# A fused attention and FFN kernel: blocks of a row-tile pair stored one by one, activation sums on VectorE, part of a weight difference in a place of its own, q and k staged by turns, statistics put later

## The chip, the cores and the metric

The kernel runs on one core of a Trainium2 chip. The metric is device time in microseconds (us) of one execution; smaller is better. Most executions of one kernel lie within 0.3% of each other. "Span" is the time from the first to the last instruction of the profiled execution, some 2 us less than the device time.

In the lines of the profile PE is TensorE's matmuls, PEld its weight loads, DVE is VectorE, ACT ScalarE, POOL GpSimd and SP SyncE; a q behind the name marks the engine's queue, which issues DMAs or waits. L1114 is a line of the kernel's source; the same statement has other line numbers in other kernels. A line of a timeline gives the start, the time taken, what ran (x3: three of them) and, in brackets, how long the engine sat idle before it and what ended that. A line of waits gives the sum in us, how often, and the longest.

## The reference, cut to what matters

```python
def _attn_ref(q, k, v):                       # 8 batches, 12 heads, 448 rows, 64 per head
    scores = np.matmul(q, k.transpose(0, 1, 3, 2)) / np.sqrt(64)
    attn = np.maximum(scores, 0.0) ** 2 / 448
    return np.matmul(attn, v)

def _moe_ref(x, g_ln, w_ch1, w_ch2):          # x: (8, 448, 768)
    mu = np.mean(x, axis=-1, keepdims=True)
    var = np.mean((x - mu) ** 2, axis=-1, keepdims=True)
    xn = (x - mu) / np.sqrt(var + 1e-06) * g_ln
    ch = np.maximum(xn @ w_ch1, 0.0) @ w_ch2  # 768 -> 3072 -> 768
    return x + ch
```

## The kernel before

While one batch goes through the FFN, the attention of the next is dealt out between its matmuls. A small scheduler inside the program gives each piece of work an assumed cost, chooses an engine for it, and writes every engine's instructions in the resulting order; each engine then works in that order. So every change of a dependency deals the work out anew, far beyond the place of the change.

The words used below: scores are the products of q and k, followed by a relu and a square; h is the FFN's hidden layer; centering subtracts a row's mean, and a scaling by g follows it; an evacuation takes a result of TensorE out of PSUM, on VectorE or ScalarE, and so frees its bank.

The second FFN matrix is cut into four quarters b11, b12, b21, b22. From the third batch on, row tiles are taken in pairs, and a pair is multiplied with seven products (P1 to P7, 12 matmuls each) where the plain way has eight. This needs sums of weights (T1 to T4, made once) and of activations (S1 to S4, made for each pair). T1 is b12 minus b11:

```python
def s_op(u, m, name, part, deps):              # an activation sum, 6 rows of hidden units
    def emit(eng):
        (nc.vector if eng == "DVE" else nc.gpsimd).tensor_sub(o, i0, i1)
    return R.add(("DVE", "POOL"), (540.0, 1700.0), emit, deps, key=-2.9, port=True)

for k in range(0, KH, 3):                      # T1 over b12, all 12 rows
    made["T1", k] = run(b12[:, k:k + 3], b12[:, k:k + 3], b11[:, k:k + 3], True, ...)

def ffn_2(u, m, j, part, parts):               # the single row tile beside a pair (once in each even batch)
    ks = [(k, w2[:, k, j * hd:(j + 1) * hd]) for k in range(K2)]
    if u > 0 and j == 1:                       # b12 is gone: add b11 back, 36 matmuls for 24
        ks = [(k, b11[:, k]) for k in range(KH)] + ks
```

The pair's products share two PSUM banks. VectorE evacuates a bank after each product (`evac`). The blocks C11 and C12 of the first tile are stored together; the blocks C22 and C21 of the second tile go one after the other through one half-tile buffer:

```python
elif key in ("p5", "C21"):
    o_t = o_half.tile([P, hd], fp32, tag="oh")          # one buffer
...
ev = evac("C22", 1, hi, r2, True, [e["p5"]])
half_free[0] = store_tile(u, m + 1, hi, ev, False, lambda: e["o", 1])
...
ev = evac("C21", 1, lo, r2, False, [half_free[0]])      # after C22's store has landed
```

q and k of a batch are loaded by GpSimd into the two halves of a staging tile and then turned by a DMA transpose from SyncE. The statistics of a batch's rows (on VectorE) and their square root (on ScalarE) may run as soon as the rows are there.

## Time and profile before

| | before |
|---|---|
| time, median of four runs | 539.01 us (538.92 to 539.26) |
| TensorE busy | 517.1 of 537.3 us |
| TensorE idle in the first 30 us | 9.55 us |
| TensorE idle from 30 us to the last matmul | 6.54 us |
| after the last matmul | 4.14 us |

TensorE is the bound. The three kinds of idleness are read from the table of stretches, with a cut at 30 us and one at the last evacuation. The first and the last are filling and emptying. The middle is where waits cost; it is 0.05 us more than the prediction's 6.49, which left out the smallest stretches. The prediction below shows the lines.

### The profile page before, as it was taken

The page shows a single profiled execution, that of the slowest core. Times are in us where ns is not written, and L with a number is a line of the kernel's source. Part 1 is how long each engine was busy: PE and PEld are TensorE (multiplying, and loading weights), DVE is VectorE, ACT ScalarE, POOL GpSimd, SP SyncE. Part 2 cuts the span into 40 slices and gives each one's busy share as a digit, 9 for nine tenths or more (in the row PEclk, how much of TensorE's full clock was granted, in tenths as well). Part 3 has the DMA queues.
Part 4 walks back from the last instruction along what each step waited for, and adds up shares of the span by engine and source line. Part 5 has one row for each costly group of instructions (what it writes and reads, how often), then busy time and mean ns, then how long its engine had stood idle before and what let it go on. Part 6 is the DMA issues. An engine that isn't in the chain of part 4 may idle for free.

```text
span 537.3 us, 9903 instructions
## 1 busy us (share of the span) xinstructions
PE 517.1 (96%) x4128; PEld 278.8 (52%) x4128; DVE 341.8 (64%) x617; ACT 231.3 (43%) x370; POOL 125.2 (23%) x137
## 2 busy tenths in 40 slices
PE   4899999999999999999988999999998999999996
PEld 3444455555564455555544545655555455554564
DVE  5988647448987588665686666746668646633253
ACT  5977611134225653366223663346441565124300
POOL 6411600311460123421172010702222012101000
PEclk9999999999999999999999999999999999999999
DMA  9999999897299004990069900992022400231022
GB/s 187 196 189 195 198 188 165 117 142 134 47 186 187 1 2 68 185 152 1 1 115 159 147 2 1 162 190 52 2 47 71 97 1 1 59 67 23 1 60 59
DMA packets 142680, 51.82 MB, mean 96 GB/s; under 512 B 121510, under 2 KB 139436, under 8 KB 142636
## 3 DMA queue, kind: packets, MB, share of 16 engines
q0 software_dynamic: 81072, 25.50, 45.1%
q1 hardware_dynamic: 55724, 14.79, 17.7%
q10 hardware_dynamic: 5840, 10.92, 7.4%
q8 instruction: 32, 0.52, 0.4%
q14 instruction: 12, 0.10, 0.1%
HBM read 51.91 MB, written 11.01 MB: 117 GB/s over the span
## 4 chain that ended last, share of the span: by engine, by line
PE 90%; DVE 5%; DMA 2%; ACT 1%; issue 1%; SPq 0%; ACTq 0%; DVEq 0%
PE f_ps L929 40%; PE f_ps L1114 20%; PE f_ps L1190 16%; PE sc L586 6%; PE ps L648 5%; DVE a L840 1%; DMA f<-in_k_dram 1%; DVE a L610 1%; DMA out_dram<-o_t 1%; DVE o_t L1128 1%; ACT a L595 1%; PE ps L507 1%; DVE t L365 0%; PE f_ps L909 0%; DVE a L849 0%
## 5 line engine op out<-in xcount | busy, mean ns | idle before, releaser
L929 PE MATMUL f_ps<-a,w 128*128 128x448 bf16 x1134 | 220.9, 353 | 1.8 <-DVE o_t L1128 1.1
L929 PEld LDWEIGHTS <-w 128*128 128x128 bf16 x1134 | 108.3, 98 | 110.3 <-issue 12.5
L595 ACT ACTIVATE a<-sc 128x896 bf16<-128x896 f32 x114 | 99.9, 923 | 85.6 <-PE sc L586 79.8
L945 ACT ACTIVATE h<-f_ps 128x448 bf16<-128x448 f32 (+1 forms) x161 | 86.0, 535 | 103.9 <-PE f_ps L929 102.4
L610 DVE TENSOR_TENSOR a<-a 128x896 bf16<-128x896 bf16 x156 | 99.0, 668 | 3.1 <-ACT a L595 2.8
L1114 PEld LDWEIGHTS <-h 128*128 128x128 bf16 x648 | 62.8, 98 | 48.7 <-issue 7.5
L1114 PE MATMUL f_ps<-w,h 128*128 128x384 bf16 x432 | 75.6, 326 | 4.4 <-DVE o_t L1128 4.4
L597 DVE TENSOR_SCALAR a<-sc 128x896 bf16<-128x896 f32 x45 | 48.9, 1087 | 24.5 <-PE sc L586 24.4
L1190 PE MATMUL f_ps<-w,h 128*128 128x384 bf16 x372 | 62.1, 326 | 0.0
L586 PE MATMUL sc<-t 64*64 64x448 bf16 x672 | 48.4, 365 | 3.3 <-ACT a L595 1.6
L1190 PEld LDWEIGHTS <-h 128*128 128x128 bf16 x372 | 36.0, 98 | 25.2 <-issue 1.7
L739 POOL TENSOR_TENSOR sum_t<-sum_t,xT_all 128x384 f32<-128x384 f32 (+2 forms) x25 | 20.4, 815 | 99.0 <-ACT xT_all L363 99.0
L1074 DVE TENSOR_TENSOR x_all<-h 128x768 bf16<-128x768 bf16 x18 | 9.9, 562 | 38.5 <-ACT h L945 38.5
L1128 DVE SCALAR_TENSOR_TENSOR o_t<-f_ps,r_t,x_all 128x384 f32<-128x384 f32 x36 | 22.1, 615 | 18.8 <-PE f_ps L1114 14.9
L586 PEld LDWEIGHTS <-t 64*64 64x64 bf16 x672 | 17.6, 106 | 26.5 <-issue 20.1
L737 POOL TENSOR_TENSOR sum_t<-xT_all 128x384 f32<-128x384 bf16 (+2 forms) x13 | 9.2, 720 | 88.9 <-ACT xT_all L363 88.8
L648 PE MATMUL ps<-a,v_t 64*64 64x448 bf16 x552 | 29.8, 350 | 0.0
L847 ACT ACTIVATE a<-a,g_sb 128x448 bf16<-128x448 bf16 x27 | 16.1, 657 | 31.2 <-DVE a L840 30.1
L1128 DVE SCALAR_TENSOR_TENSOR o_t<-f_ps,r_t,o_t 128x384 f32<-128x384 f32 x27 | 16.6, 615 | 19.4 <-PE f_ps L1114 19.2
L363 ACT CAST xT_all<-ps 128x768 bf16<-128x768 f32 (+2 forms) x33 | 20.2, 622 | 20.1 <-PE ps L648 18.3
L401 POOL DMA_DIRECT2D t<-in_q_dram x12 | 19.3, 1774 | 36.1 <-DMA t<-t 34.6
L648 PEld LDWEIGHTS <-v_t 64*64 64x64 bf16 x672 | 19.7, 107 | 13.4 <-issue 2.8
(91 smaller groups left out, 420.2 us busy)
## 6 DMA issues: line engine op xcount, KB each, us to landing
out_dram<-o_t ACTq DMA_DIRECT2D x38, 192.0 KB, 4.7
v_t<-in_v_dram POOLq DMA_DIRECT2D x16, 336.0 KB, 6.3
w<-in_moe_w_ch_dram POOLq DMA_DIRECT2D x4, 1152.0 KB, 40.0
t<-in_q_dram POOLq DMA_DIRECT2D x12, 336.0 KB, 8.3
t<-in_k_dram POOLq DMA_DIRECT2D x12, 336.0 KB, 10.5
out_dram<-o_t ACTq DMA_DIRECT2D x35, 96.0 KB, 2.2
w<-in_moe_w_ch_dram POOLq DMA_DIRECT2D x4, 768.0 KB, 19.2
w<-in_moe_w_ch_dram POOLq DMA_DIRECT2D x1, 1536.0 KB, 29.2
```

What stands on the lines that cost most here:

```text
L363: nc.scalar.copy(o, i)
L586: nc.tensor.matmul(sc[rows_of(half), r, :S], qkT[b][rows_of(r), 1, s * NPER + pn, rows_of(half)], qT[:, :, pn, rows_of(half)], start=True, ...
L595: nc.scalar.activation(attn[n, s], st[0][:, :, :S], Act.Relu, scale=rc2)
L597: nc.vector.tensor_scalar(attn[n, s], st[0][:, :, :S], rc2, 0.0, op0=Alu.mult, op1=Alu.max)
L610: nc.vector.tensor_mul(attn[n, s], attn[n, s], attn[n, s])
L648: nc.tensor.matmul(av_st[n][half][rows_of(hh)], vt[b][rows_of(half), 2 * pn + hh, s * D:(s + 1) * D], attn[n, s][rows_of(half), hh, :], st ...
L739: nc.gpsimd.tensor_add(s0, s0, x0)
L929: nc.tensor.matmul(st[0], w1[:, ki, ni * P:(ni + 1) * P], xc[b][:, ki, :], start=(i == 0), stop=(i == K1 - 1))
L945: nc.scalar.activation(o, st[0][:, c], Act.Relu)
L1114: nc.tensor.matmul(e["ps", bank], a(k), w(k), start=new and k == 0, stop=k == KH - 1, skip_group_check=True)
L1128: nc.vector.scalar_tensor_tensor(o, e["ps", bank], r, o if more else xm[u, m + tile_n][:, cols], op0=Alu.mult, op1=Alu.add)
L1190: nc.tensor.matmul(o_st["ps"], stat(u, m, ki), w, start=(i == 0), stop=(i == len(ks) - 1))
```

## The change

The intent: take matmuls away where b11 had to be added back, and take away the waits of TensorE in the middle. Cut to its core:

```diff
@@ q and k staged by turns: from batch 4 both use the first half of the staging tile
-                        stage[b][half * T:(half + 1) * T, t]...
+                        stage["cols"][half * T:(half + 1) * T, t if b < 4 else 0]...
-                ld.append(load(dma_ns(6 * S, 256), emit, free, 2000.0))
+                ld.append(load(dma_ns(6 * S, 256), emit, free if t == 0 or b < 4 else [later("turn", b, 0)], 2000.0))
@@ statistics and square root later
-            sto = R.add("DVE", 1400.0, stats, [deps_of[m], ops.get(("st0", b))], key=4.0)
+            sto = R.add("DVE", 1400.0, stats, [deps_of[m], ops.get(("st0", b)), later("h", b, 4) if u > 0 else None], key=4.0)
-        sq = R.add("ACT", 300.0, root, [ops["st", u, m] for m in ms], key=3.0)
+        sq = R.add("ACT", 300.0, root, [ops["st", u, m] for m in ms] + [later("h", b, 14) if u > 0 else None], key=3.0)
@@ seven rows of T1 in the second half of the staging tile, five over b12
-        for k in range(0, KH, 3):
-            made["T1", k] = run(b12[:, k:k + 3], b12[:, k:k + 3], b11[:, k:k + 3], True,
+        for k in range(J):                      # J = 7
+            tw["T1", k] = stage["cols"][:, 1, k]
+        for a, z in ((0, 3), (3, 5), (5, J)):
+            made["T1", a] = run(stage["cols"][:, 1, a:z], b12[:, a:z], b11[:, a:z], True, ...)
+        for k, n in ((J, 3), (J + 3, 2)):
+            made["T1", k] = run(b12[:, k:k + n], b12[:, k:k + n], b11[:, k:k + n], True,
...
-            ks = [(k, b11[:, k]) for k in range(KH)] + ks
+            ks = [(k, b11[:, k]) for k in range(J, KH)] + ks
@@ activation sums on VectorE
-        return R.add(("DVE", "POOL"), (540.0, 1700.0), emit, deps, key=-2.9, port=True)
+        return R.add("DVE", 570.0, emit, deps, key=-2.9, port=True)
@@ blocks stored one by one, C21 in the left half of the first tile's output
-                elif key in ("p5", "C21"):
+                elif key == "p5":
+            e["C11 out"] = store_tile(u, m, lo, ev, False, lambda: e["o", 0][:, lo])
-            o_ring.append(store_tile(u, m, slice(0, d_model), ev, False, lambda: e["o", 0]))
+            e["C12 out"] = store_tile(u, m, hi, ev, False, lambda: e["o", 0][:, hi])
-            ev = evac("C21", 1, lo, r2, False, [half_free[0]])
+            ev = evac("C21", 1, lo, r2, False, [e["C11 out"]])
```

More of the change, by code (lines that the diff above doesn't have):

```diff
@@ L392, in load_qk_cols @@
     def load_qk_cols(b):
-        free = [ops["qk_free", 0]] if b == 2 else [ops["turn", b - 1, x] for x in range(2)]
+        free = [ops["qk_free", 0]] if b == 2 else [later("turn", b - 1, x) for x in range(2)]
         for t, src in enumerate((q, k)):
@@ L398, in emit @@
                 def emit(eng, t=t, src=src, half=half):
-                    if half == 0 and t == 0:
-                        stage[b] = big(STAGE[b], None, t=2, j=J, c=hd)
+                    if half == 0 and t == 0 and b == 2:
+                        stage["cols"] = big(STAGE[b], None, t=2, j=J, c=hd)
                     nc.gpsimd.dma_start(
-                        stage[b][half * T:(half + 1) * T, t].rearrange("p j (h d) -> p j h d", d=D),
+                        stage["cols"][half * T:(half + 1) * T, t if b < 4 else 0].rearrange("p j (h d) -> p j h d", d=D),
                         src[b, half * 6:half * 6 + 6].rearrange("h (p j) d -> p j h d", j=J))
-                ld.append(load(dma_ns(6 * S, 256), emit, free, 2000.0))
+                ld.append(load(dma_ns(6 * S, 256), emit, free if t == 0 or b < 4 else [later("turn", b, 0)], 2000.0))
             ops["c_ld", b, t] = ld
@@ L414, in emit @@
                 nc.sync.dma_start_transpose(
-                    qkT[b][:, t], stage[b][:, t].rearrange("p j c -> p (j c)"))
+                    qkT[b][:, t], stage["cols"][:, t if b < 4 else 0].rearrange("p j c -> p (j c)"))
             ops["turn", b, t] = R.add("SP", 100.0, emit, ops["c_ld", b, t] + [ops[free]],
                                       key=0.0, load=(J * NPER * P, 18.0))
+            now_known(ops["turn", b, t], "turn", b, t)
     w1_view = moe_w_ch1.rearrange("(ko kp) n -> kp ko n", kp=P)
@@ L1035, in make_sums @@
                                         tw["T2", k + i].rearrange("p (o c) -> p o c", o=1), True, [made["T2", k + i]] + d, 5.2)
-        for k in range(0, KH, 3):
-            made["T1", k] = run(b12[:, k:k + 3], b12[:, k:k + 3], b11[:, k:k + 3], True,
+        for k in range(J):
+            tw["T1", k] = stage["cols"][:, 1, k]
+        for a, z in ((0, 3), (3, 5), (5, J)):
+            made["T1", a] = run(stage["cols"][:, 1, a:z], b12[:, a:z], b11[:, a:z], True,
+                                w2_ld + [later("turn", 3, 1)], 5.3)
+        for k, n in ((J, 3), (J + 3, 2)):
+            for i in range(k, k + n):
+                tw["T1", i] = b12[:, i]
+            made["T1", k] = run(b12[:, k:k + n], b12[:, k:k + n], b11[:, k:k + n], True,
                                 done3 + [later("f2_end", 0)], 5.3)
@@ L1101, in ffn_w @@
         bank = "x" if name in ("P1", "P6", "P7", "P4") else "y"
-        w = {"P1": lambda k: b11[:, k], "P2": lambda k: b21[:, k], "P6": lambda k: tw["T2", k], "P5": lambda k: b12[:, k],
+        w = {"P1": lambda k: b11[:, k], "P2": lambda k: b21[:, k], "P6": lambda k: tw["T2", k], "P5": lambda k: tw["T1", k],
              "P7": lambda k: tw["T3", k], "P3": lambda k: b22[:, k], "P4": lambda k: tw["T4", k]}[name]
@@ L1123, in emit @@
                     e["o", 0] = o_t
-                elif key in ("p5", "C21"):
+                elif key == "p5":
                     o_t = o_half.tile([P, hd], fp32, tag="oh")
                     e["o", 1] = o_t
-                o = e["o", 1] if tile_n else e["o", 0][:, cols]
+                o = e["o", 1] if key in ("p5", "C22") else e["o", 0][:, cols]
                 nc.vector.scalar_tensor_tensor(o, e["ps", bank], r, o if more else xm[u, m + tile_n][:, cols],
@@ L1137, in ffn_w @@
             e["S4"] = [s_op(u, m, "S4", x, [op, e["S2"][x]]) for x in range(2)]
-            evac("C11", 0, lo, r1, True, [e["c1"]])
+            ev = evac("C11", 0, lo, r1, True, [e["c1"]])
+            e["C11 out"] = store_tile(u, m, lo, ev, False, lambda: e["o", 0][:, lo])
         elif name == "P6":
@@ L1154, in ffn_w @@
             ev = evac("C12", 0, hi, r1, True, [e["c2"], e["C11"]])
-            o_ring.append(store_tile(u, m, slice(0, d_model), ev, False, lambda: e["o", 0]))
+            e["C12 out"] = store_tile(u, m, hi, ev, False, lambda: e["o", 0][:, hi])
         else:
-            ev = evac("C21", 1, lo, r2, False, [half_free[0]])
+            ev = evac("C21", 1, lo, r2, False, [e["C11 out"]])
             f_banks[:] = [e["C12"], ev]
             f_tags.reverse()
-            half_free[0] = store_tile(u, m + 1, lo, ev, final, lambda: e["o", 1])
+            o_ring.append([e["C12 out"], store_tile(u, m + 1, lo, ev, final, lambda: e["o", 0][:, lo])])
             if m == 3:
@@ L1165, in ffn_w, with part_of @@
                 now_known(op, "f2_end", b)
+    def part_of(u, j, part, parts):
+        n = K2 if u == 0 or j == 0 else K2 + KH - J
+        return slice(part * n // parts, (part + 1) * n // parts)
     def f2_deps(u, m, j, part, parts):
-        n = (K2 if u == 0 or j == 0 else 3 * KH) // parts
         b = 2 * u + (0 if m < 3 else 1)
-        z = min((part + 1) * n, K2) - 1
+        z = min(part_of(u, j, part, parts).stop, K2) - 1
         d = [ops["w2", z], ops["h", b, z]]
@@ L1186, in emit @@
                 o_st["ps"] = o_ps
-            n = len(ks) // parts
-            for i in range(part * n, (part + 1) * n):
-                ki, w = ks[i]
+            for i, (ki, w) in list(enumerate(ks))[part_of(u, j, part, parts)]:
                 nc.tensor.matmul(o_st["ps"], stat(u, m, ki), w, start=(i == 0), stop=(i == len(ks) - 1))
-        op = R.pe(162.5 * len(ks) / parts, emit, f2_deps(u, m, j, part, parts) + (ops["sums", "T1"] if u > 0 and j == 1 else []))
+        run = part_of(u, j, part, parts)
+        op = R.pe(162.5 * (run.stop - run.start), emit, f2_deps(u, m, j, part, parts) + (ops["sums", "T1"] if u > 0 and j == 1 else []))
         if m in (2, 6) and j == 1 and part == parts - 1:
@@ L1300, in f2_steps @@
         return [("f2", u, m, j, p, n) for m in ms for j in range(2)
-                for n in [PARTS if u == 0 or j == 0 else 6] for p in range(n)]
+                for n in [PARTS if u == 0 or j == 0 else 5] for p in range(n)]
     def fw_steps(u, ms):
```

## The prediction

> **What bounds the kernel now.** I read four views in this order: the page's busy line, the table of stretches of 10 us, the waits of TensorE, and the timeline and chain of waits at the stretches that were not full.
>
> ```profile
> PE 517.1 (96%) x4128; PEld 278.8 (52%) x4128; DVE 341.8 (64%) x617; ACT 231.3 (43%) x370; POOL 125.2 (23%) x137
> ```
>
> TensorE works 517.1 of 537.3 us, so all that can be won is matmuls taken away, plus at most 20.2 us of idleness. The columns below are the busy time of PE, PEld, DVE, ACT and POOL in each stretch.
>
> ```profile
> 260.00:270.00 10.00, 9.98 (x97) 5.50 (x98) 7.35 (x14) 3.52 (x5) 0.00 (x0) 1.00 0.09 21
> 270.00:280.00 10.00, 9.49 (x63) 5.40 (x56) 7.92 (x11) 2.89 (x4) 8.31 (x9) 1.00 0.66 130
> 280.00:290.00 10.00, 7.94 (x48) 4.58 (x47) 7.30 (x12) 1.78 (x3) 5.45 (x4) 1.00 1.94 124
> 290.00:300.00 10.00, 8.87 (x56) 4.29 (x54) 3.62 (x7) 4.82 (x7) 0.00 (x0) 1.00 0.98 190
> ...
> 400.00:410.00 10.00, 8.20 (x51) 4.83 (x50) 8.25 (x10) 1.50 (x3) 6.11 (x7) 1.00 0.65 128
> ...
> 490.00:500.00 10.00, 9.32 (x50) 4.71 (x49) 1.91 (x6) 4.97 (x10) 0.00 (x0) 1.00 0.01 2
> ```
>
> From 30 us on, TensorE is full except here and for 0.31 us in 420 to 430. The first 30 us lose 9.55 us (loads and first transposes), the tail 4.13 us (last matmul ends at 533.17). The middle loses 0.51 + 2.06 + 1.13 + 1.80 + 0.31 + 0.68 = 6.49 us. The sum, 20.2, closes the account. The waits of TensorE in the middle name the releasers:
>
> ```profile
> PE f_ps L1114 <- DVE o_t L1128: 4.4, 3, 1.8
> PE f_ps L929 <- DVE o_t L1128: 1.1, 1, 1.1
> PE f_ps L929 <- ACT h L945: 0.7, 1, 0.7
> ```
>
> L1114 are the products of the seven-product scheme on a pair of row tiles, L1128 the evacuations of their banks. So 5.5 us are lost where a product waits for a bank. The timeline shows why, at the second pair of an odd batch (the same pattern comes again at 404 us):
>
> ```profile
> 275.49 3.55 POOL L1074 TENSOR_TENSOR h<-h,x_all 128x768 bf16<-128x768 bf16 x2 [1.37 <-PE f_ps L1114]
> 275.97 1.56 DVE L1074 TENSOR_TENSOR h<-h,x_all 128x768 bf16<-128x768 bf16 x1
> ...
> 277.46 3.25 DVE L840 TENSOR_TENSOR a<-xT_all,sum_t 128x768 bf16<-128x768 bf16 x2
> ...
> 280.64 0.60 DVE L1128 SCALAR_TENSOR_TENSOR o_t<-f_ps,r_t,o_t 128x384 f32<-128x384 f32 x1
> ...
> 281.30 2.11 PE L1114 MATMUL f_ps<-w,h 128*128 128x384 bf16 x12 [1.80 <-DVE o_t L1128]
> ```
>
> GpSimd makes two of the pair's activation sums, 1.8 us each. Beside it VectorE takes 1.56 us for a sum that has a minimum of 0.54 elsewhere, and 1.63 for a centering (L840) that takes 0.96 when alone. The evacuation, fourth in VectorE's order, ends 1.8 us too late. Later in the same stage the chain shows another wait:
>
> ```profile
> 286.82 0.47 ACTq L1228
> ...
> 287.33 5.05 DMA out_dram<-o_t
> ...
> 292.58 0.63 DVE o_t L1128
> ```
>
> The pair's last block shares one half-tile buffer with the block before the last, and waits 5.05 us for its store to land; TensorE loses 1.13 us of that.
>
> **What the Trainium skill says.** (1) "VectorE: DVE Perf Modes", section on the TRN2 errata, gives a matmul max(60, 6+FD) cycles at 2.4 GHz: 390 cycles, 162.5 ns, for 384 columns. The trace agrees: a piece of the chain has 60 of them (L1190) in 9.75 us, 162.5 ns each. The 326 ns in the groups is a latency, not the pitch. (2) "SBUF — State Buffer", section "Who interferes with whom": a VectorE instruction with two SBUF inputs contends with a GpSimd instruction that reads SBUF, and the one issued second blocks. The 1.56 and 1.63 us above agree. (3) "DMA: Bandwidth & Descriptors", "Anatomy of one DMA": about 2 us are fixed, mostly the receipt. The 96 KB stores land 2.2 us after issue in the median here; the 5.05 us came while q and k loads held the DMA engines.
>
> **The change, part by part.**
>
> *Home for seven rows of T1 (b12 minus b11).* Before, T1 overwrote b12, so the single tile of each of the three even batches after the first two had to add b11 back: 36 matmuls for its right half. Seven rows now lie in half of the staging tile, b12 stays whole there, and the half takes 24 + 5 = 29. Comparing the built instruction orders of TensorE confirms 21 fewer matmuls and 101 changes between attention and FFN work in both. 21 x 162.5 ns = **3.41 us**, in stretches where TensorE is full, so it counts whole unless the next FFN waits for its centered input. The gains before that FFN end at 348.9 us and it starts at 352.3; in the tightest of the three, 221.4 and 223.6. The mean moves six matmuls (0.98 us) earlier in the order, so most of the 1.14 us taken from each such tile comes from before it. VectorE's work for T1 hardly changes: 12 rows either way.
>
> *Sums on VectorE.* Five sums leave GpSimd (four beside the two stalls, one at 485 us) and cost VectorE 5 x 0.51 us of pitch, beside a TensorE that needs 8 us per four products. In the new order of VectorE, with pitches from the trace (evacuation 0.54, sum 0.5, centering 0.87), from the end of the first product, t: evacuation 0.54, two sums 1.54, centering 2.41, evacuation of the second product 2.95, done at 3.0; the fourth product needs it at 3.9. Two sums 3.95, a centering 4.82, third evacuation done at 5.4; the fifth product needs it at 5.86. So both waits of 1.80 us should go, and with VectorE back in time also the 0.76 us at 286. Gain 1.80 + 1.80 + 0.76 = 4.36 (the 0.51 us of stretch 270 to 280 are the beginning of the first wait).
>
> *Blocks stored one by one.* The last block goes into the left half of the output tile, whose earlier content was stored some 8 us before; the 1.13 us wait goes. Eighteen more stores of 0.55 us issue time fall on ScalarE's queue (43% busy). At the very end the block before the last sends 96 instead of 192 KB a store: about 0.2 us of tail.
>
> *Statistics later.* The square root now stands behind six more evacuations on ScalarE. At 490.4 us ScalarE sat waiting for statistics and TensorE lost 0.68 us, at 428 another 0.31. Both should go: 0.99.
>
> *q and k staged by turns, from batch 4.* k's load starts only after q's transpose. From the trace: transposes 6.4 us to landing, the two k loads about 13 us together. For batch 5: q's turn starts at 229.0, lands at 235.4, k lands at 248.5, its turn at 255; its first scores are at 268.0. Batches 4, 6 and 7 have 12 to 17 us of slack in the same way. Cost: nothing. GpSimd's row sums queue behind the k loads for up to 8 us, but only the last of three per batch is urgent, 30 us later.
>
> **Sum.** 538.98 - 3.41 (matmuls) - 4.36 (port) - 1.13 (store) - 0.99 (statistics) - 0.2 (tail) = 528.9. This is nearly a floor, since head and tail stay. For new small waits after ScalarE and VectorE were dealt out anew I add 1.2 us, a guess of the size of the small waits seen before: **530.1 us**.
>
> **Rivals.** (a) *The wait moves instead of going.* Five more sums make VectorE's order tighter just where it is fullest (about 8 of 10 us at 270 to 290); if each of the two stages keeps half its wait, 2 to 3 us come back: 532.5. For: VectorE's order is strict and the margins above are 0.4 to 0.9 us. Against: all other pairs already ran their sums there without a wait. (b) *Staging by turns is late.* If k took 26 instead of 13 us, batches 5 to 7 would arrive around or after their first scores and the greedy schedule would stall, up to several us each: 535 or more. Against: transfers of 6 to 13 us in every batch of this trace. (c) *Only the matmuls count*, the idleness being a symptom of something else such as a late mean: 535.4. Against: at 281.30 the wait is for the evacuation itself. (d) *Stores hold up ScalarE.* More issues, each waiting for an older store, delay h and the scores' relu: 1 to 3 us back.
>
> **Range and chances.** The floor is about 528.7, because 9.55 us of head and most of the 4.13 us of tail are untouched; rivals (a) and (d) together end near 533. Eight in ten: 528.9 to 533.0. A gain of 2% would need 528.2, below the floor, so faster by over 2% has 0.04; slower by over 2% would need stalls of 20 us: 0.02; within 2%: 0.94.
>
> **What would show it.** TensorE with 4107 matmuls and about 513.7 us busy; no wait of the pair products above 0.5 us; no GpSimd instruction at the line of the activation sums; centerings near 0.96 us throughout; no evacuation waiting for a store; q and k transposes done 10 us before the scores. It is wrong if scores wait for a transpose, if waits for evacuations total over 2 us, or if the gain stays at 3.4 us.

## The result

The changed kernel takes **530.47 us** (median of four runs, 530.28 to 530.81) against 539.01 us before. The ratio is 0.9842, with a 95% interval of 0.9825 to 0.9859. Ratios here are the mean time of one kernel's fast runs over that of the other's of the same rounds, so they are not quite the ratio of the medians. It is 1.6% faster, within the 2% that counts as the same.

The page's busy line of the changed kernel, then its table of stretches (busy time of PE, PEld, DVE, ACT, POOL): around 280 and 400 us, where before had its largest gaps, and around its own largest, at 363 us:

```profile
PE 513.4 (97%) x4107; PEld 276.9 (52%) x4107; DVE 341.5 (65%) x632; ACT 227.0 (43%) x361; POOL 117.3 (22%) x132
```

```profile
270.00:280.00 10.00, 10.00 (x63) 6.00 (x62) 8.27 (x14) 1.48 (x3) 5.72 (x7) 1.00 1.44 162
280.00:290.00 10.00, 10.00 (x68) 5.44 (x66) 7.13 (x15) 3.60 (x5) 0.00 (x0) 1.00 0.72 116
290.00:300.00 10.00, 9.71 (x84) 4.97 (x83) 6.56 (x13) 7.04 (x12) 4.13 (x4) 1.00 0.88 130
...
350.00:360.00 10.00, 9.77 (x92) 4.75 (x91) 6.54 (x16) 7.70 (x14) 2.45 (x2) 1.00 0.81 132
360.00:370.00 10.00, 9.40 (x51) 4.76 (x50) 5.54 (x9) 5.67 (x11) 2.33 (x3) 1.00 1.43 136
...
400.00:410.00 10.00, 10.00 (x63) 6.03 (x62) 8.36 (x17) 1.23 (x2) 0.00 (x0) 1.00 0.21 55
```

Twenty-one matmuls are gone, and the gaps around 280 and 400 us with them. The waits of TensorE between 30 and 522 us are now only these:

```profile
PE sc L587 <- ACT a L596: 1.1, 4, 0.3
PE f_ps L930 <- DVE h L948: 0.6, 1, 0.6
```

No product (L1122 in the changed kernel, L1114 before) waits for an evacuation (L1136, before L1128) any more. The timeline at the place of the first 1.80 us wait:

```profile
274.03 0.62 DVE L1136 SCALAR_TENSOR_TENSOR o_t<-f_ps,r_t,x_all 128x384 f32<-128x384 f32 x1 [0.27 <-PE f_ps L1122]
...
274.56 1.02 DVE L1082 TENSOR_TENSOR h<-h,x_all 128x768 bf16<-128x768 bf16 x2
275.50 0.95 DVE L841 TENSOR_TENSOR a<-xT_all,sum_t 128x768 bf16<-128x768 bf16 x1
...
276.37 0.61 DVE L1136 SCALAR_TENSOR_TENSOR o_t<-f_ps,r_t,o_t 128x384 f32<-128x384 f32 x1
...
278.70 0.61 DVE L1136 SCALAR_TENSOR_TENSOR o_t<-f_ps,r_t,x_all 128x384 f32<-128x384 f32 x1
```

Two sums now take 1.02 us together and a centering 0.95. The second evacuation starts 2.34 us after the first (the prediction laid it at 2.41), the third ends at 5.28 (predicted 5.4).

The span went from 537.3 to 528.6 us, by 8.7: TensorE's busy time fell by 3.7, its idleness in the middle from 6.54 to 1.77 us (4.77), the head by 0.57, and the tail grew by 0.32. The head is no gain of the change: the two instruction orders of TensorE are the same for the first 150 us, and over all fourteen profiles the head lies between 8.6 and 10.1 us.

### The profile page after: what moved, and what is told of

It is laid out like the page before. It is cut to its first block, busy times and chain, and to the rows that moved or that the text cites. A ratio compares the mean times of both kernels' runs of the same rounds, so it can differ in the third digit from the quotient of the medians.

```text
span 528.6 us, 9882 instructions
## 1 busy us (share of the span) xinstructions
PE 513.4 (97%) x4107; PEld 276.9 (52%) x4107; DVE 341.5 (65%) x632; ACT 227.0 (43%) x361; POOL 117.3 (22%) x132
## 4 chain that ended last, share of the span: by engine, by line
PE 93%; DVE 4%; ACT 1%; DMA 1%; issue 0%; ACTq 0%; DVEq 0%
PE f_ps L930 40%; PE f_ps L1122 23%; PE f_ps L1200 15%; PE sc L587 6%; PE ps L649 5%; DVE a L611 2%; ACT a L596 1%; DVE t L365 1%; DMA f<-in_q_dram 1%; PE ps L508 1%; PE f_ps L910 0%; PE ps L711 0%; DVE st L792 0%; DVE st L791 0%; PE f_ps L508 0%
## 5 line engine op out<-in xcount | busy, mean ns | idle before, releaser
L596 ACT ACTIVATE a<-sc 128x896 bf16<-128x896 f32 x117 | 103.4, 927 | 81.9 <-PE sc L587 75.9
L946 ACT ACTIVATE h<-f_ps 128x448 bf16<-128x448 f32 (+1 forms) x156 | 83.2, 534 | 106.5 <-PE f_ps L930 105.2
L611 DVE TENSOR_TENSOR a<-a 128x896 bf16<-128x896 bf16 x156 | 100.6, 683 | 1.4 <-ACT a L596 1.4
L1122 PEld LDWEIGHTS <-h 128*128 128x128 bf16 x648 | 62.8, 98 | 43.8 <-issue 2.4
L598 DVE TENSOR_SCALAR a<-sc 128x896 bf16<-128x896 f32 x42 | 45.6, 1087 | 41.2 <-PE sc L587 41.1
L1122 PE MATMUL f_ps<-w,h 128*128 128x384 bf16 x369 | 65.2, 326 | 0.0
L1200 PE MATMUL f_ps<-w,h 128*128 128x384 bf16 x351 | 58.7, 326 | 0.0
L1200 PEld LDWEIGHTS <-h 128*128 128x128 bf16 x351 | 33.9, 98 | 23.8 <-issue 1.7
L1136 DVE SCALAR_TENSOR_TENSOR o_t<-f_ps,r_t,x_all 128x384 f32<-128x384 f32 x36 | 22.1, 614 | 18.6 <-PE f_ps L1122 18.3
L401 POOL DMA_DIRECT2D t<-in_k_dram x12 | 20.0, 1901 | 52.7 <-DMA t<-t 52.7
L1217 DVE SCALAR_TENSOR_TENSOR o_t<-f_ps,r_t,x_all 128x384 f32<-128x384 f32 x20 | 12.3, 613 | 26.4 <-PE f_ps L1200 26.3
L1136 DVE SCALAR_TENSOR_TENSOR o_t<-f_ps,r_t,o_t 128x384 f32<-128x384 f32 x27 | 16.6, 614 | 14.8 <-PE f_ps L1122 14.7
L848 ACT ACTIVATE a<-a,g_sb 128x448 bf16<-128x448 bf16 x19 | 11.6, 659 | 30.3 <-DVE a L841 15.1
```

What stands on the lines that cost most here:

```text
L401: nc.gpsimd.dma_start(stage["cols"][half * T:(half + 1) * T, t if b < 4 else 0].rearrange("p j (h d) -> p j h d", d=D), src[b, half * 6:ha ...
L596: nc.scalar.activation(attn[n, s], st[0][:, :, :S], Act.Relu, scale=rc2)
L598: nc.vector.tensor_scalar(attn[n, s], st[0][:, :, :S], rc2, 0.0, op0=Alu.mult, op1=Alu.max)
L611: nc.vector.tensor_mul(attn[n, s], attn[n, s], attn[n, s])
L946: nc.scalar.activation(o, st[0][:, c], Act.Relu)
L1122: nc.tensor.matmul(e["ps", bank], a(k), w(k), start=new and k == 0, stop=k == KH - 1, skip_group_check=True)
```

## The experiments

Twelve kernels ran, all correct. Each part was run alone on the kernel before, and each was taken out of the changed kernel; "staging by turns" can stand without the home, not the home without it. The edits of the first nine are hunks of the diff above: *alone* is the kernel before plus the named hunks, *without* the changed kernel minus them. The table gives the ratio to before with its interval, and from each one's profile TensorE's idleness by the method of the table before.

```
kernel                     label    median us  ratio to before          middle  tail
before                     -        539.01     1                         6.54   4.14
changed                    -        530.47     0.9842 [0.9825, 0.9859]   1.77   4.46
home + staging alone       f_t1     537.06     0.9962 [0.9949, 0.9976]   7.63   4.18
sums alone                 f_sops   535.39     0.9925 [0.9907, 0.9942]   3.34   4.17
stores alone               f_store  538.13     0.9986 [0.9967, 1.0005]   5.88   4.41
statistics alone           f_stats  538.41     0.9987 [0.9972, 1.0003]   6.11   4.25
staging alone              f_stage  539.91     1.0012 [0.9998, 1.0026]   6.65   4.14
without home               r_t1     535.20     0.9920 [0.9907, 0.9933]   2.66   4.41
without sums               r_sops   533.34     0.9888 [0.9873, 0.9902]   4.54   4.41
without stores             r_store  531.27     0.9848 [0.9835, 0.9861]   2.89   4.17
without late statistics    r_stats  533.86     0.9902 [0.9885, 0.9918]   4.32   4.48
k loaded twice             k_twice  531.48     0.9857 [0.9844, 0.9871]   1.50   4.41
only the root late         v_root   532.15     0.9868 [0.9855, 0.9882]   3.02   4.46
bias for evacuations       v_evac   531.21     0.9852 [0.9837, 0.9867]   1.17   4.46
```

### The home for seven rows of T1

> The kernel before with only the home for seven T1 rows and the staging by turns that makes room for it. Theory (21 matmuls fewer, at a place where TensorE is full): 21 x 162.5 ns = 3.4 us, so 535.6 us, with the two waits of 1.80 us for the evacuation and the store wait of 1.13 us still in the trace, because GpSimd still makes its sums and the half tile is still shared. Rival (the time of the right half does not count because the centered input comes late): within 1 us of before. Rival (any new dealing of work dissolves the waits): 531 to 533.

> The changed kernel without the home for the seven T1 rows (T1 again over b12, 36 matmuls for the right half of the single tiles), all else as changed, also the staging by turns. Theory: 21 matmuls come back into full TensorE, 3.4 us, 533.9 us; fewer new waits than the home brought when it stood alone, because the statistics now stay late. Rival (the home is worth only the 2.1 us that it gave alone): 532.5.

Alone it gave 0.38% (2 us), not 3.4. The matmuls are gone in full: the six profiles with 4128 matmuls have a mean TensorE busy time of 517.5 us, the eight with 4107 have 513.6, that is 3.9 less, where 21 x 162.5 ns is 3.4. The chain of before and then of the changed kernel shows it at one single tile:

```profile
341.88 9.75 PE f_ps L1190 x60
```

```profile
336.77 8.61 PE f_ps L1200 x53
```

Seven matmuls fewer are 1.14 us. But alone, the middle grew from 6.54 to 7.63 us: the waits of TensorE list 3.4 us for evacuations of h (1.9 by ScalarE, 1.5 by VectorE), which were 0.7 before. Of the old waits the two of 1.80 us stayed, as expected, but the one of 0.76 us and that for the store, which should have stayed too, were gone; the part on the staging comes back to this. Taken out of the changed kernel, the home was missed by 0.8% (0.9920 less 0.9842, 4.2 us, where 3.4 were expected); 0.9 us of that is a longer middle, 2.66 for 1.77 us. Nothing waits there for ScalarE's evacuations of h, and 1.4 us for VectorE's. So the term was of the right size. That the late statistics are what lets it count in full fits these runs, but no run has only these two parts.

### The activation sums

> The kernel before with only the activation sums moved to VectorE. Theory (port): both waits of 1.80 us and the 0.76 us go, 4.4 us in all, so 534.6; no GpSimd instruction at the line of the sums, every centering near 0.95 us, and the store wait of about 1 us stays. Rival (the wait moves to the next evacuation because VectorE has more to do): 536 to 538.

> The changed kernel with the activation sums again on VectorE or GpSimd. Theory: the sums of the second pair go to GpSimd again, and the waits for evacuations of 1.80 us come back, 3.5 to 4.5 us: 534 to 535. Rival (with the other parts in place GpSimd gets no sums or they do no harm): 530.5 to 531.

Alone: the product waits of 4.4 us are gone, as the theory says. The waits of TensorE in its middle that are over 0.3 us:

```profile
PE f_ps L929 <- ACT h L945: 1.7, 1, 1.7
PE f_ps L929 <- DVE o_t L1128: 1.3, 1, 1.3
```

The second is the store wait, which stays as expected. The first was 0.7 before; it grew by 1.0 us and ate part of the gain, which came to 4.0 us by the ratio (535.39 us, where 534.6 was expected). Without them, the two product waits are back, first in the waits of TensorE and then in the groups:

```profile
PE f_ps L1122 <- DVE o_t L1136: 3.6, 2, 1.8
```

```profile
L1082 POOL TENSOR_TENSOR h<-h,x_all 128x768 bf16<-128x768 bf16 x4 | 7.1, 1794 | 2.8 <-PE f_ps L1122 2.8
```

Four sums on GpSimd, two waits of 1.8 us, in the same stretches (270 and 400 us) as before. The port theory holds in both directions for these two waits. But only 2.5 us were lost (0.9888 less 0.9842), where 3.5 to 4.5 were expected: the third product wait of before, 0.76 us at 286, did not come back, and the changed kernel's 0.6 us for an evacuation of h went.

### The stores

> The kernel before with only the blocks stored one by one. Theory: only the store wait goes, 1.1 us, so 537.9; the two 1.80 us waits stay. Rival (the 18 extra stores hold up ScalarE): 539 to 541.

> The changed kernel with the old stores (one for a whole row tile, and a shared half tile for the two late blocks). Theory: one wait for the half tile's store comes back for each pair in which loads run beside it, 1.1 to 1.4 us as before: 531.7. Rival: q alone is loaded at that time now, the store lands sooner and nothing comes back: 530.5.

Alone, the wait of 1.1 us for the store is gone and the 4.4 us of product waits stay; the intervals do not separate the gain of about 0.8 us from nothing. Without them, a store wait comes back, but at another pair, at 217 us (timeline):

```profile
216.69 0.62 DVE L1136 SCALAR_TENSOR_TENSOR o_t<-f_ps,r_t,x_all 128x384 f32<-128x384 f32 x1 [4.48 <-DMA out_dram<-o_t]
...
217.37 1.95 PE L1199 MATMUL f_ps<-w,h 128*128 128x384 bf16 x11 [0.96 <-DVE o_t L1136]
```

VectorE stands 4.48 us for the half tile's store, and TensorE loses 0.96. The time differs from that of the changed kernel by less than the intervals. Where before had its wait, at 293 us, none comes back, as the rival said: the staging by turns alone already removes it, with the old stores (below). So in the whole, the gain of this part is not shown.

The tails in the table say one more thing: with the new stores they are 4.41 to 4.48 us in all eight profiles, with the old ones 4.14 to 4.25 in all six. SyncE's last wait differs in the same way, shown for before and then for the changed kernel:

```profile
SPq L1494 <- DMA out_dram<-o_t: 1.5, 2, 1.1
```

```profile
SPq L1505 <- DMA out_dram<-o_t: 1.8, 1, 1.8
```

So the new stores cost 0.3 us at the end. The last block's own store takes the same 2.4 us to land; why the end then waits longer was not tested and stays open.

### The late statistics

> The kernel before with only the statistics and the square root put later. Theory: 0.68 us at 490 and 0.31 at 428 go, and a wait of about 0.6 us may come where the statistics now meet the squares on VectorE, as in the changed kernel at 363 us; so 538.0 to 538.7. Rival (it matters more, because the statistics crowd VectorE at the pairs): 536 or less.

> The changed kernel with the statistics and the square root as early as before. Theory: the wait of an h evacuation behind the square root, which grew to 1.26 us with the home alone and to 1.7 with the sums alone, comes back and the 0.6 us at 363 goes: 1.5 to 3 us worse, 532 to 533.5. Rival (the part is worth what it gave alone, 0.7 us): 531.2.

> The changed kernel with the statistics as early as before and only the square root late. Theory (the wait at 480 us is ScalarE standing in order behind the square root, whose statistics are late): this wait of 1.44 us stays away although the statistics are early, so about 531 to 532; waits for h evacuations by VectorE remain. Rival (the early statistics on VectorE are what costs): 533 to 534, as with both early.

The edit of the last, against the changed kernel:

```diff
-            sto = R.add("DVE", 1400.0, stats, [deps_of[m], ops.get(("st0", b)), later("h", b, 4) if u > 0 else None], key=4.0)
+            sto = R.add("DVE", 1400.0, stats, [deps_of[m], ops.get(("st0", b))], key=4.0)
```

Alone this part gave 0.7 us (not clear of nothing), but the changed kernel without it is 0.6% slower, 3.2 us (533.86 us; 532 to 533.5 were expected). Its timeline shows the wait:

```profile
484.53 0.30 ACT L801 ACTIVATE r_t<-mv_t,eps_sb 128x4 f32<-128x4 f32 x1 [2.29 <-DVE mv_t L793]
...
485.31 0.92 PE L930 MATMUL f_ps<-a,w 128*128 128x448 bf16 x4 [1.44 <-ACT h L946]
```

ScalarE stands 2.29 us before the square root, whose statistics are late, with an evacuation of h behind it, and TensorE loses 1.44 us. (The Trainium skill, "Perfetto Trace Analysis", section "Tensor Engine Instruction", calls ScalarE, VectorE and GpSimd strict first-in, first-out; the trace agrees, the evacuation ran only after the root.) The same wait was 0.68 us before, 1.26 with home and staging alone, 1.70 with the sums alone, 0.95 with the stores alone, but 0.40 with the staging alone: it can take back a part of what another part wins. That fits the parts' gaining 7.5 us together when each stood alone (the sum of 0.38, 0.75, 0.14 and 0.13% of 539), and 8.5 at once; the intervals are too wide to show that difference.

The other half of the expectation failed: with the early statistics the wait for VectorE's evacuation near 363 us did not go (0.81 us at 361.5, and 0.91 at 240.5), and the late statistics alone do not bring it. It belongs to the staging, next section; the late statistics rather shorten it.

With only the root late, the wait for ScalarE stays away, so it belongs to the root's place. But 1.8 us of waits for VectorE's evacuations of h remain (0.6 in the changed kernel), and the time, 0.9868 (532.15 us), lies between. That points to both halves doing work, though its interval still touches that of the changed kernel.

### Staging by turns

> The kernel before with only q and k staged by turns; T1 still over b12, so no matmul is saved. The home alone gave 2.1 us where 3.4 were due. Theory A: the 1.3 us are the price of staging by turns (k's descriptors and the row sums behind them run on GpSimd later, beside squares on VectorE): about 540.3 us, with waits for h evacuations near 240 and 363 us. Theory B (my prediction: staging costs nothing, the loss is only in how VectorE and ScalarE were dealt out anew): within 0.4 us of before.

> The changed kernel with each k of batches 4 to 7 loaded twice into the same place (the same values), so that it is there some 6 to 8 us later. Prediction: slack of 12 to 17 us before the first scores, so no wait of scores for a transpose, within 1 us of the changed kernel, 530.5 to 531.5. Rival (staging is at its limit): several us worse, 533 or more, with scores waiting for the transpose.

```diff
                 ld.append(load(dma_ns(6 * S, 256), emit, free if t == 0 or b < 4 else [later("turn", b, 0)], 2000.0))
+                if t == 1 and b >= 4:
+                    ld.append(load(dma_ns(6 * S, 256), emit, [later("turn", b, 0)], 2000.0))
```

With k loaded twice, batch 7's last piece of k is issued at 373.09 us, some 12 us later than in the changed kernel if both are counted from their own q loads, and its scores still start at 392.44 without a wait (timelines of GpSimd and TensorE):

```profile
373.09 1.59 POOL L401 DMA_DIRECT2D t<-in_k_dram  x1 [5.23 <-DMA t<-in_k_dram]
```

```profile
392.44 0.14 PEld L589 LDWEIGHTS <-t 64*64 64x64 bf16 x8 [0.32 <-issue]
```

The slack was real, and no score waits for a transpose. Staging alone came out at 1.0012, between the two theories, with an interval that holds 1, no change. Its trace shows both a cost and a gain that theory B did not have. In the waits of TensorE one of 1.5 us for VectorE's evacuation of h appears, at 367 us. The changed kernel has its largest wait at the same place:

```profile
357.55 3.21 POOL L401 DMA_DIRECT2D t<-in_k_dram  x2 [20.48 <-DMA t<-t]
...
358.12 5.24 DVE L611 TENSOR_TENSOR a<-a 128x896 bf16<-128x896 bf16 x6
...
360.04 2.29 POOL L738 TENSOR_TENSOR sum_t<-xT_all 128x384 f32<-128x384 bf16 x2
...
363.28 0.61 DVE L948 TENSOR_SCALAR h<-f_ps 128x448 bf16<-128x448 f32 x1
...
363.94 2.24 PE L930 MATMUL f_ps<-a,w 128*128 128x448 bf16 x11 [0.60 <-DVE h L948]
```

GpSimd waits 20.48 us for q's transpose, issues k, and only then makes the row sum, beside six squares on VectorE; one of them takes 1.68 us instead of 0.57. The evacuation of h stands behind the squares. In the kernel before, at this point of the same batch, GpSimd was free, took one of the squares itself and made its sums in half the time:

```profile
363.44 1.68 POOL L612 TENSOR_TENSOR a<-a 128x896 bf16<-128x896 bf16 x1 [16.23 <-ACT a L595]
365.37 1.18 POOL L737 TENSOR_TENSOR sum_t<-xT_all 128x384 f32<-128x384 bf16 x2 [0.26 <-ACT xT_all L363]
```

The run with k loaded twice bears this out: there GpSimd waits to issue the second load and makes no row sum at this place, four squares take 2.18 us (0.55 each), and the 0.60 us wait is gone.

The gain: with the staging alone, two waits are gone that the prediction had put down to other parts, the product wait of 0.76 us at 286 and the 1.13 us for the store, though GpSimd still makes its sums and the half tile is still shared. The product wait came from a scaling on VectorE. The timelines of before and of the staging alone:

```profile
281.48 3.97 POOL L401 DMA_DIRECT2D t<-in_k_dram  x2
...
283.49 2.05 DVE L849 TENSOR_SCALAR a<-a,g_sb 128x448 bf16<-128x448 bf16 x3
```

```profile
286.03 0.81 DVE L850 TENSOR_SCALAR a<-a,g_sb 128x448 bf16<-128x448 bf16 x3
```

Beside GpSimd's issuing of k's load one of the three scalings took 1.34 us, where the median of all is 0.33, and the evacuation behind them was late. The same is seen with the stores alone and with the statistics alone (1.34 and 1.36 us); in the runs where k's load comes later no scaling takes over 0.52 us (0.34 with the staging alone), even without the sums part. (With the sums alone the scalings ran only after that load had been issued, so that part removes this wait as well.) The store that took 5.05 us was in flight beside k's load, too. So the staging alone removes 1.9 us of waits and brings about as much in new ones: the middle is 6.65 us, where it was 6.54.

### An attempt at something better

> The changed kernel with a bias of 500 ns against VectorE in the choice of the engine for h evacuations from batch 2 on, so that these stand behind squares less often. Theory: the wait of 0.60 us at 363 goes, so 529.9 and a little faster than the changed kernel; if ScalarE is then late for scores' relu, it gains nothing: 530.5 to 531.

```diff
-        ev = R.add(("ACT", "DVE"), (560.0, 620.0) if b != 1 else (750.0, 740.0), relu, [op], key=-3.0)
+        ev = R.add(("ACT", "DVE"), (560.0, 620.0) if b != 1 else (750.0, 740.0), relu, [op], key=-3.0, bias={"DVE": 500.0} if b > 1 else None)
```

The 0.60 us wait is gone, the middle is down to 1.17 us, and the profiled span is 528.1 against 528.6 us. But the timed runs go from 529.91 to 531.65 us, and the ratio, 0.9852, is that of the changed kernel within the intervals. A gain of half a microsecond was not shown; the changed kernel stays the best.

## Why the prediction was right

The prediction said 530.1 us, 528.9 to 533.0; it was 530.47. By its steps:

- **Matmuls, 3.41 us: right.** 21 fewer, 3.7 us less busy time in the two profiles compared, 1.14 us at each single tile. Rival (c), that only this counts, falls with the middle's 4.77 us.
- **Sums on VectorE, 4.36 us: right for 3.60.** The order of VectorE ran within 0.12 us of the working, all product waits went, and the two of 1.80 us came back when the sums were given back to GpSimd. The 0.76 us had another cause: the evacuation at 286 was late because a scaling before it ran beside the issuing of k's load. The sums alone and the staging alone each remove it. Rival (a), the wait that only moves within the pair, falls: no product waits.
- **Stores, 1.13 us: the wait went, but perhaps not through this part.** No evacuation of a product waits for a store in the changed kernel; but the staging alone removes this wait too, and without the new stores the time is the same within the intervals. Rival (d) falls: the waits for scores' relu are 1.1 us in all.
- **Statistics, 0.99 us: half right.** The 0.68 us at 490 went. The 0.31 us at 428 was no matter of the statistics: it stays in the run with the statistics alone (0.32), and the trace there has scores waiting for ScalarE's relu, 0.29 in three places of the changed kernel. The prediction put it to the statistics only because both lay in one stretch. It also took this part for a small one; it is worth 3.2 us once the others are in.
- **Tail, 0.2 us to win: wrong in sign.** 0.3 us were lost.
- **Staging costs nothing: right for what was feared, incomplete.** Rival (b), late scores, falls even with k loaded twice. It takes away the 0.76 and the 1.13 us by itself, which the prediction did not see. And GpSimd's later work now runs beside VectorE's squares and delays evacuations of h, 0.6 us in the changed kernel.
- **1.2 us for new small waits: about right.** The changed kernel's middle has 1.77 us, of which 0.31 were there before.

In sum the prediction had 8.9 us: 3.41 for the matmuls, 5.28 for the middle (4.36, 1.13 and 0.99, less 1.2 for new waits) and 0.2 for the tail. The profiles show 8.7: 3.7, 4.77, a tail longer by 0.32, and a head shorter by 0.57. The head is luck, and it covers the errors of middle and tail; without it the time would have been about 531.0 us, still in the range. Putting two waits down to the wrong parts cost nothing, because the parts that remove them were all in the change.

## What to carry to other kernels

Close the account of the bounding engine's idleness first (head, middle, tail), and name each wait of the middle; the sum of the named waits is then both the forecast and its floor. When a change has several parts on strictly ordered engines, do not add up what each gives alone: a wait left in place can grow as others vanish (0.68 to 1.70 us here), and one wait can be removed by either of two parts, so take each part out of the whole as well. Where two engines slow each other, as VectorE and GpSimd do here, taking one job off GpSimd is a gain only if no other job is then moved beside VectorE's work.

## What the Trainium skill lacked or had wrong

- "SBUF — State Buffer", "Who interferes with whom", agrees with the runs in kind (second to issue blocks) but gives no figure for two instructions with two SBUF inputs each. Here a VectorE sum of 0.54 us took 1.56 beside one of 1.8 us on GpSimd, and GpSimd's pair of row sums took 2.29 instead of 1.18 us beside VectorE's squares: both sides lose.
- The same section leaves as inferred that a VectorE instruction with two SBUF inputs is not slowed by descriptor making on GpSimd. The changed kernel does not settle it: squares issued at 172.81, 234.79 and 298.00 us beside k's load took 0.57 to 0.62 us, one at 358.60 beside another took 1.33.
- "DMA: Bandwidth & Descriptors", "Anatomy of one DMA": its about 2 us of fixed cost are given for DMAs that GpSimd issues. The stores here are issued by ScalarE; those of 96 KB took 2.2 us to landing in the median, and one beside loads in flight took 5.05 us, for which that section has no measure.
- None of the pages read says that splitting the last stores can lengthen the end: 4.41 to 4.48 us after the last matmul with 96 KB stores, 4.14 to 4.25 with 192 KB ones, cause open.
